# Local attention with a convolved feed-forward: attn @ v and scores of tile pairs as one TensorE step, on two lent PSUM banks

## The chip, the cores and the metric

The kernel runs on one core of a Trainium2 chip. A core has TensorE (PE in the profile; its weight loads are listed as PEld), VectorE (DVE), ScalarE (ACT), GpSimd (POOL) and SyncE (SP), which issues the DMAs here. The matrix products land in PSUM, which has eight banks of 512 fp32 columns on 128 partitions. The metric is device microseconds of one execution; the time of a kernel is the median of several runs.

## The reference

```
# q, k, v: 8 batches x 8 heads x 576 rows x 64;  d_model 512, d_ff 1024
chunk = 64                                  # attention inside chunks of 64 rows
scores = scale * q_c @ k_c^T
attn = exp(scores - max(scores))
attn = attn / (sum(attn) + 1e-9)
x = concat_heads(attn @ v_c)                # (8, 576, 512)

h = relu(x @ w_in)                          # (8, 576, 1024)
conv = sum over k in 0..2 of conv_w[k] * h shifted by k - 1 rows   # zero at the ends
out = (h * sigmoid(conv)) @ w_out           # (8, 576, 512)
```

All inputs and the output are fp32.

## The kernel before

**Tiles.** The 8 x 576 rows are cut in 36 tiles of 128 rows, two chunks of 64 rows with all 8 heads each. Of a tile, q and k come in transposed: up to tile 8 by PE transposes (`t_pe`, L144) and ACT copies, from tile 9 on by DVE (`t_dve`, L155). `scores` (L163) is a block of 16 matmuls of 64 x 64 x 64, which the profile lists as 32 records. Then come the maximum (`s_max`, DVE, L181), the subtraction (`s_sub`, DVE, L185), the exponential (ACT, L190), the sum, eps and reciprocal (DVE, L194 to L200), the product (POOL, L203), four PE transposes of the probabilities (`p_pe`, L210) with an ACT copy (L215), and `attn_v` (L217), another block of 16 small matmuls in 32 records. The result x, transposed, is split into a high and a low part: `x_hi` (ACT, L247) and `x_lo` (DVE, L251).

**Units.** The feed-forward runs on 16 units of 288 rows (half a batch). For each of the 8 slices of 128 features, `mm1` (L254) is a block of 12 matmuls (high x high, low x high, high x low, over 4 slices of d_model) with 290 columns. Its PSUM bank goes through `h_relu`, `c_mid` (ACT), `c_left`, `c_right` (DVE), `c_sig` (ACT) and `c_mul` (DVE, L290), which gives the bank back; `g_hi` (ACT) and `g_lo` (POOL, L304) split the gated rows. `mm2` (L309) multiplies by w_out: for each of 36 output tiles, 8 slices of 3 matmuls with 512 columns, all into one bank, which `o_copy` (ACT, L318) empties. The weights are split into high and low parts by DVE, ACT and POOL in the first part of the kernel (L327 to L379).

**PSUM.** `sx` is one tile of two banks, in two halves (`sx_half`, L160). A half holds the scores or the x of one tile, in 256 columns of both banks. Six more banks (`banks`) are shared by mm1, mm2 and all PE transposes.

**Order.** Every piece of work is a `step` with an engine, a cost, a due time (`key`), what must precede it, and the buffers that it takes and frees (`room`, L394). A planner (L583 to L677) goes through time and chooses, for each engine, the next step by due time. It adds a cost when PE turns between three kinds of work (`kinds`, `turn`: big matmuls, the small blocks of scores and attn_v, transposes), and it draws a small block to another one by six microseconds of due time (L632). Tables (`by_step_early` for due times under 110, `by_step`, `by_chain`) shift the due times. The instructions are then issued in the planned order, which each engine keeps. Where the plan leaves PE idle before the first mm2, filler transposes of the identity are put in (L685). In `att` (L424), a tile's chain of steps is written down from the load to `x_lo`.

Of the kernel before, what the change touches and what calls it, by code (L numbers as in the profile page):

```python
# [30 lines left out]
def attn_ffn(ctx: ExitStack, tc: tile.TileContext, q, k, v, w_in, conv_w, w_out, out):  # L31
    nc = tc.nc
# [17 lines left out]
    TG = 3  # L50
    scale = 1.0 / float(D) ** 0.5
# [108 lines left out]
    def sx_half(i):  # L160
        return sx[:, :, G * C * i:G * C * i + G * C]

    def scores(st):  # L163

        s_ps = sx_half(st["s"])
        qT, kT = st[0], st[1]
        for g in range(G):
            for s in range(2):
                for hp in range(2):
                    d0 = 64 * hp  # L170
                    nc.tensor.matmul(  # L171
                        s_ps[C * s:C * s + C, hp ^ s, C * g:C * g + C],
                        lhsT=qT[d0:d0 + D, g, C * s:C * s + C],
                        rhs=kT[d0:d0 + D, g, C * s:C * s + C],
                        start=True, stop=True,
                    )

    def s_max(st):
        st["sv"] = sx_half(st["s"]).rearrange("p u (g j) -> p u g j", j=C)
        st["m"] = work.tile([P, 2, G], F32, name="m")  # L180
        nc.vector.tensor_reduce(out=st["m"], in_=st["sv"], op=ALU.max, axis=AX.X)  # L181

    def s_sub(st):
        st["e"] = work.tile([P, H, C], F32, name="e")
        nc.vector.tensor_tensor(  # L185
            out=st["e"].rearrange("p (g u) j -> p u g j", u=2), in0=st["sv"],
            in1=st["m"].rearrange("p u (g o) -> p u g o", o=1).broadcast_to([P, 2, G, C]), op=ALU.subtract)
# [29 lines left out]
    def attn_v(st):  # L217
        x_ps = sx_half(st["x"])
        for g in range(G):
            for s in range(2):  # L220
                for hp in range(2):
                    j0 = 64 * (hp ^ s)
                    nc.tensor.matmul(  # L223
                        x_ps[D * hp:D * hp + D, s, C * g:C * g + C],
# [4 lines left out]

    def x_views(st, t, x):  # L230

        xv = sx_half(st.get("x", 0)).rearrange("p s (g i) -> p g s i", i=C)
# [7 lines left out]
        if [p[1:4] for p in parts] == [(0, C, parts[0][3])] * 2:  # L240
            _, _, _, u, o = parts[0]
            return [(xv, x[:, u, :, o:o + 2 * C].rearrange("p g (s i) -> p g s i", i=C))]
        return [(xv[:, :, s, i:i + n], x[:, u, :, o:o + n]) for s, i, n, u, o in parts]
# [150 lines left out]
    room = {"slot": 2, "wslot": 2, "sx": 2, "bk": 6, "grp": 2, "v": 4, "qT": 2, "kT": 2, "m": 2, "e": 2, "z": 2, "pT": 2, "c": 7, "wt": 2,  # L394
# [29 lines left out]
    def att(t, key, load_key, writes):  # L424
# [19 lines left out]
        s = step("PE", 0.47, key, scores, (st,), tt + [before.get("s")], take=[("sx", st, "s")], free=["qT", "kT"], bank="sx")  # L444
        before.update(v=ldv, T=tt[1], s=s)
# [8 lines left out]
        s = step("ACT", 0.59, key + 12, p_copy, (st,), [s], take=["pT"], free=[("bk", "pt")])  # L454
        s = step("PE", 0.47, key + 14, attn_v, (st,), [s, ldv], take=[("sx", st, "x")], free=["pT", "v"], bank="sx")
        n = len(x_views(st, t, x_h)) - 1
        s = step("ACT", 0.58 + 0.15 * n, key + 14, x_hi, (st, t), [s] + writes, bank="sx")
        return step("DVE", 0.69 + 0.1 * n, key + 14, x_lo, (st, t), [s], free=[("sx", "x")], bank="sx")

    group_loads, before = {}, {}  # L460
# [57 lines left out]

    for u in range(NU + 1):

        for t in tiles_for[u] if u < NU else []:
# [3 lines left out]
            x_done[t] = att(t, key_of[t], 0.1 + 0.5 * t if t < 5 else 4.5 + t, writes)  # L525
# [23 lines left out]
        "w_load": -4.5, "w_mask": -6, "w_bias": -5.5, "w_rest": -5, "w_low": -2, "w_sign": -9.5, "w_pow": -6,  # L549
        "<lambda>": -7, "c_sum": -23.5, "c_pe": 5, "c_copy": -31.5, "w_hi": 12, "w_lo_big": 20, "load_rows": -11,  # L550
        "t_pe": -7.5, "t_copy": -11, "load_v": 10.5, "scores": -3, "s_max": 8, "s_sub": -21.5, "s_exp": -9, "s_sum":
        -0.5, "s_eps": 2.5, "s_rec": 10, "s_norm": -19, "p_copy": -0.5, "attn_v": 4, "x_hi": -3, "x_lo": -6, "mm1":
        -0.5, "h_relu": -4.5, "c_mid": 2, "c_left": 2.5, "c_right": 2.5, "c_sig": 5, "c_mul": 6, "g_hi": 3, "g_lo":
        29.5, "o_copy": 6, "o_store": 16.5, "load_group": 35.5, "load_part": -3.5, "t_dve": 23
    }
    by_step = {
        "w_load": -4.5, "w_mask": -6, "w_bias": -5.5, "w_rest": -5, "w_low": -2, "w_sign": -9.5, "w_pow": -6,
        "<lambda>": -7, "c_sum": -23.5, "c_pe": 5, "c_copy": -31.5, "w_hi": 12, "w_lo_big": 20, "load_rows": -11,
        "t_pe": -7.5, "t_copy": -11, "load_v": 10.5, "scores": -3, "s_max": 8, "s_sub": -21.5, "s_exp": -9, "s_sum":
        -0.5, "s_eps": 2.5, "s_rec": 10, "s_norm": -19, "p_copy": -0.5, "attn_v": 4, "x_hi": -3, "x_lo": -6, "mm1":  # L560
        -0.5, "h_relu": -4.5, "c_mid": 2, "c_left": 2.5, "c_right": 2.5, "c_sig": 5, "c_mul": 6, "g_hi": 3, "g_lo":
        29.5, "o_copy": 6, "o_store": 16.5, "load_group": 35.5, "load_part": -3.5, "t_dve": 23
    }
    by_chain = [
# [155 lines left out]
```

## Time and profile before

| | |
|---|---|
| median of 3 runs | 516.65 us (516.14 to 516.67) |
| the profiled execution | 517.22 us |
| its span, first to last instruction | 515.4 us |
| TensorE clock granted, mean | 0.999 |
| mm2 matmuls (L313) | 864, 344.3 us busy in three groups |
| mm1 matmuls (L260) | 1536, 271.5 us busy in three groups |
| attn_v records (L223) and scores records (L171) | 1152 each, 24.5 and 24.3 us |
| filler transposes (L685) | 183, 26.0 us |
| DMA queue, share of the 16 engines | 40.5% |

The profile is of one execution. "Busy" of an engine counts its instructions' times without gaps; matmuls overlap, so the sums of the PE groups exceed the time that PE takes for them, and what a matmul costs is read from the distance between starts. A row of the timeline gives the start, the length, the engine, the line, the operation, its output and inputs, and how many neighbours it merges; a row of the waits gives who waited for whom, the total in us, how many times, and the longest.

### The profile page before, as it was taken

The page shows a single profiled execution, that of the slowest core. Times are in us where ns is not written, and L with a number is a line of the kernel's source. Part 1 is how long each engine was busy: PE and PEld are TensorE (multiplying, and loading weights), DVE is VectorE, ACT ScalarE, POOL GpSimd, SP SyncE. Part 2 cuts the span into 40 slices and gives each one's busy share as a digit, 9 for nine tenths or more (in the row PEclk, how much of TensorE's full clock was granted, in tenths as well). Part 3 has the DMA queues.
Part 4 walks back from the last instruction along what each step waited for, and adds up shares of the span by engine and source line. Part 5 has one row for each costly group of instructions (what it writes and reads, how often), then busy time and mean ns, then how long its engine had stood idle before and what let it go on. Part 6 is the DMA issues. An engine that isn't in the chain of part 4 may idle for free.

```text
span 515.4 us, 13095 instructions
## 1 busy us (share of the span) xinstructions
PE 505.4 (98%) x5104; PEld 450.8 (87%) x5104; DVE 351.8 (68%) x732; ACT 325.1 (63%) x783; POOL 172.1 (33%) x237
## 2 busy tenths in 40 slices
PE   8898999999999999999999999999999999999997
PEld 8788988888998899899888898889889898988985
DVE  5779999668749588867854499727858585753320
ACT  4678998845866367757635487737746567755430
POOL 1424485532314323532511153314313315043220
PEclk9999999999999999999999999999999999999999
DMA  8889751543325545523455554343551211001101
GB/s 218 198 218 262 187 131 37 93 100 88 51 46 117 89 114 108 98 47 51 100 114 113 123 89 85 57 97 74 97 121 33 61 23 42 2 1 43 41 14 68
DMA packets 183170, 47.04 MB, mean 91 GB/s; under 512 B 175404, under 2 KB 175428, under 8 KB 183108
## 3 DMA queue, kind: packets, MB, share of 16 engines
q1 hardware_dynamic: 183108, 46.20, 40.5%
q8 instruction: 40, 0.66, 0.6%
q14 instruction: 22, 0.18, 0.1%
HBM read 36.72 MB, written 9.44 MB: 90 GB/s over the span
## 4 chain that ended last, share of the span: by engine, by line
PE 85%; DVE 8%; DMA 3%; ACT 2%; POOL 1%; issue 0%; SPq 0%; DVEq 0%; ACTq 0%; POOLq 0%
PE b_ps L313 38%; PE b_ps L260 37%; PE sx_ps L223 4%; PE sx_ps L171 3%; DMA qk<-in_moe_w_in 3%; PE b_ps L210 3%; DVE wt L360 1%; DVE wv L355 1%; POOL wv L376 1%; DVE wv L351 1%; DVE we L368 1%; DVE c L281 1%; DVE wt L342 1%; DVE c L290 1%; DVE x_l L251 1%; DVE c L275 1%
## 5 line engine op out<-in xcount | busy, mean ns | idle before, releaser
L304 POOL TENSOR_TENSOR g_l<-c,g_h 128x288 fp32r<-128x288 f32 (+8 forms) x184 | 114.7, 638 | 217.3 <-ACT g_h L300 209.8
L313 PE MATMUL b_ps<-wo_h,g_h 128*128 128x512 f32 x288 | 118.1, 410 | 0.0
L313 PE MATMUL b_ps<-wo_h,g_l 128*128 128x512 f32 x288 | 113.3, 393 | 0.0
L313 PE MATMUL b_ps<-wo_l,g_h 128*128 128x512 f32 x288 | 112.9, 392 | 0.0
L275 DVE SCALAR_TENSOR_TENSOR c<-b_ps,cw,c 128x288 f32<-128x288 f32 (+1 forms) x128 | 65.2, 512 | 62.7 <-ACT c L271 62.4
L260 PE MATMUL b_ps<-x_h,wi_h 128*128 128x290 f32 x512 | 91.5, 300 | 1.3 <-DVE c L290 1.3
L260 PE MATMUL b_ps<-x_l,wi_h 128*128 128x290 f32 x512 | 90.2, 298 | 0.0
L260 PE MATMUL b_ps<-x_h,wi_l 128*128 128x290 f32 x512 | 89.8, 297 | 0.0
L260 PEld LDWEIGHTS b_ps<-x_h,wi_h 128*128 128x128 f32 x512 | 77.3, 189 | 6.2 <-DVE c L290 2.3
L266 ACT ACTIVATE b_ps<-b_ps 128x290 f32<-128x290 f32 x128 | 50.7, 398 | 47.1 <-PE b_ps L260 46.4
L300 ACT CAST g_h<-c 128x288 fp32r<-128x288 f32 (+8 forms) x184 | 60.3, 358 | 26.9 <-DVE c L290 13.3
L260 PEld LDWEIGHTS b_ps<-x_h,wi_l 128*128 128x128 f32 x512 | 76.4, 190 | 0.0
L260 PEld LDWEIGHTS b_ps<-x_l,wi_h 128*128 128x128 f32 x512 | 76.3, 189 | 0.0
L290 DVE SCALAR_TENSOR_TENSOR c<-c,b_ps 128x288 f32<-128x288 f32 x128 | 57.2, 449 | 20.5 <-ACT c L287 18.8
L287 ACT ACTIVATE c<-c 128x288 f32<-128x288 f32 x128 | 56.5, 443 | 22.7 <-DVE c L281 21.5
L281 DVE SCALAR_TENSOR_TENSOR c<-b_ps,cw,c 128x287 f32<-128x287 f32 (+1 forms) x128 | 65.4, 514 | 2.9
L271 ACT ACTIVATE c<-b_ps,cw 128x288 f32<-128x288 f32 x128 | 63.3, 498 | 4.7 <-POOL g_l L304 0.4
L313 PEld LDWEIGHTS b_ps<-wo_h,g_l 128*128 128x128 f32 x288 | 54.1, 188 | 12.2
L203 POOL TENSOR_TENSOR e<-e,z 128x512 f32<-128x512 f32 x36 | 38.1, 1062 | 75.8 <-DVE z L200 62.5
L313 PEld LDWEIGHTS b_ps<-wo_h,g_h 128*128 128x128 f32 x288 | 54.2, 188 | 10.3
L313 PEld LDWEIGHTS b_ps<-wo_l,g_h 128*128 128x128 f32 x288 | 54.2, 188 | 8.6
L181 DVE TENSOR_REDUCE m<-sx_ps 128x8 f32<-128x512 f32 x36 | 24.6, 683 | 22.3 <-PE sx_ps L171 21.4
(48 smaller groups left out, 513.1 us busy)
## 6 DMA issues: line engine op xcount, KB each, us to landing
v<-in_v SPq DMA_DIRECT2D x144, 64.0 KB, 2.6
out<-wt SPq DMA_DIRECT2D x36, 256.0 KB, 2.4
qk<-in_q SPq DMA_DIRECT2D x96, 48.0 KB, 2.3
qk<-in_k SPq DMA_DIRECT2D x96, 48.0 KB, 2.3
qk<-in_moe_w_out SPq DMA_DIRECT2D x4, 1024.0 KB, 7.7
qk<-in_q SPq DMA_DIRECT2D x96, 24.0 KB, 1.9
qk<-in_k SPq DMA_DIRECT2D x96, 24.0 KB, 1.9
qk<-in_moe_w_in SPq DMA_DIRECT2D x4, 512.0 KB, 5.1
```

Source lines behind the costliest of these rows:

```text
L181: nc.vector.tensor_reduce(out=st["m"], in_=st["sv"], op=ALU.max, axis=AX.X)
L203: nc.gpsimd.tensor_tensor(out=st["e"], in0=st["e"], in1=st["z"].rearrange("p (h o) -> p h o", o=1).broadcast_to([P, H, C]), op=ALU.mult)
L260: nc.tensor.matmul(h_ps[:, 0:XU], lhsT=wt[:, f // 2, kt, P * (f % 2):P * (f % 2) + P], rhs=xt[:, u % NX, kt, :], start=n == 0, stop=n == 3 ...
L266: nc.scalar.activation(out=banks[st["h"]][:, 0:XU], in_=banks[st["h"]][:, 0:XU], func=AF.Relu)
L271: nc.scalar.mul(out=st["c"], in_=banks[st["h"]][:, i0:i0 + HS], mul=cw[:, FT + f:FT + f + 1])
L275: nc.vector.scalar_tensor_tensor(out=c[:, a:HS], in0=banks[st["h"]][:, i0 + a - 1:i0 + HS - 1], scalar=cw[:, f:f + 1], in1=c[:, a:HS], op0 ...
L281: nc.vector.scalar_tensor_tensor(out=c[:, 0:b], in0=banks[st["h"]][:, i0 + 1:i0 + 1 + b], scalar=cw[:, 2 * FT + f:2 * FT + f + 1], in1=c[: ...
L287: nc.scalar.activation(out=st["c"], in_=st["c"], func=AF.Tanh, scale=0.5)
L290: nc.vector.scalar_tensor_tensor(out=st["c"], in0=st["c"], scalar=1.0, in1=banks[st["h"]][:, st["i0"]:st["i0"] + HS], op0=ALU.add, op1=ALU ...
L300: nc.scalar.copy(out=g_h[:, f, gs], in_=st["c"][:, cs])
L304: nc.gpsimd.tensor_tensor(out=g_l[:, f, gs], in0=st["c"][:, cs], in1=g_h[:, f, gs].bitcast(F32), op=ALU.subtract)
L313: nc.tensor.matmul(banks[st["o"]], lhsT=gt[:, f, o:o + P], rhs=wt[:, f, :], start=f == 0 and n == 0, stop=f == FT - 1 and n == 2)
```

## The change

Tiles 0 to 11 keep a step each for scores, and tiles 0 to 10 for attn_v. From tile 12 on, two tiles (12 and 13, 14 and 15, ...) are taken together: `both` is one step of PE that holds attn_v of the two tiles before (in the first one, of tile 11 alone) and then scores of the two new ones. Attn_v of tiles 34 and 35 is one last step. Softmax (`soft`) and the split of x (`x_steps`) stay steps of single tiles.

The four blocks need four places. From tile 11's scores on, two of the six shared banks are taken for good (`give_up`, which issues nothing) and make two more halves, numbers 0 and 1; halves 2 and 3 are the old `sx`. As a lent pair is two separate tiles, `sx_half` returns two views there, and `s_max`, `s_sub`, `x_hi` and `x_lo` issue an instruction for each bank.

Units of x are now filled in when mm1 first needs them (the loop with `begun`). All tables of due times are replaced; the one for due times of 110 and more is empty. Fillers may stand wherever the plan leaves PE idle up to 110 us. A bank that is not given back counts as held to the end.

```
+    BOTH = 12
+    PAIR = 12
...
     def sx_half(i):
-        return sx[:, :, G * C * i:G * C * i + G * C]
+        cols = slice(G * C * (i % 2), G * C * (i % 2) + G * C)
+        if i // 2:
+            return [(slice(0, 2), sx[:, :, cols])]
+        return [(slice(u, u + 1), banks[lent["y", u]].rearrange("p (u n) -> p u n", u=1)[:, :, cols]) for u in range(2)]
+
+    def sx_bank(i, u):
+        parts = sx_half(i)
+        return parts[0][1][:, u, :] if len(parts) == 1 else parts[u][1][:, 0, :]
...
     def s_max(st):
-        st["sv"] = sx_half(st["s"]).rearrange("p u (g j) -> p u g j", j=C)
         st["m"] = work.tile([P, 2, G], F32, name="m")
-        nc.vector.tensor_reduce(out=st["m"], in_=st["sv"], op=ALU.max, axis=AX.X)
+        for us, sv in sx_half(st["s"]):
+            nc.vector.tensor_reduce(out=st["m"][:, us], in_=sv.rearrange("p u (g j) -> p u g j", j=C), op=ALU.max, axis=AX.X)
...
+    def both(st, tiles, tiles_x):
+        for a in tiles_x:
+            attn_v(a)
+        for a in tiles:
+            scores(a)
...
-    room = {"slot": 2, "wslot": 2, "sx": 2, "bk": 6, "grp": 2, "v": 4, "qT": 2, "kT": 2, "m": 2, "e": 2, "z": 2, "pT": 2, "c": 7, "wt": 2,
+    room = {"slot": 2, "wslot": 2, "sx": 4, "bk": 6, "grp": 2, "v": 4, "qT": 2, "kT": 2, "m": 2, "e": 2, "z": 2, "pT": 2, "c": 7, "wt": 2,
...
-        s = step("PE", 0.47, key, scores, (st,), tt + [before.get("s")], take=[("sx", st, "s")], free=["qT", "kT"], bank="sx")
-        before.update(v=ldv, T=tt[1], s=s)
+        before.update(v=ldv, T=tt[1])
+        before["new"].append((st, t, tt, ldv, writes, key))
+        if t >= PAIR and (t - PAIR) % 2 == 0:
+            return
+        new, old = before["new"], before["x"] if t >= BOTH else []
+        before["new"], key = [], new[0][5]
+        after = [a for n in new for a in n[2]] + [before.get("s")] + [a for o in old for a in o[2]]
+        take = [("sx", o[0], "x") for o in old] + [("sx", n[0], "s") for n in new]
+        free = ["qT", "kT"] * len(new) + ["pT", "v"] * len(old)
+        if old:
+            s = step("PE", 0.47 * len(new + old), key, both, (new[0][0], [n[0] for n in new], [o[0] for o in old]), after,
+                     take=take, free=free, bank="sx")
+        else:
+            s = step("PE", 0.47, key, scores, (st,), after, take=take, free=free, bank="sx")
+        before["s"] = s
+        for b, tb, _, writes_b in old:
+            x_steps(b, tb, s, key, writes_b)
+        if t == PAIR - 1:
+            a = step("POOL", 0.0, key, give_up, (lent,), [s], take=[("bk", lent, ("y", 0))])
+            step("POOL", 0.0, key, give_up, (lent,), [a], take=[("bk", lent, ("y", 1))], free=[("sx", "l0"), ("sx", "l1")])
+        before["x"] = [(st_, t_, soft(st_, s, key + 4 * n) + [v_], w_) for n, (st_, t_, _, v_, w_, _) in enumerate(new)]
+        if t + 1 < BOTH:
+            x_alone(key + 14)
+        elif t == NT - 1:
+            x_alone(key + 18)
...
-        for t in tiles_for[u] if u < NU else []:
+        while begun < NT and u < NU and not all(t in x_done for t in range(until[u])):
+            t, begun = begun, begun + 1
...
-    kinds = {scores: 1, attn_v: 1, p_pe: 2, t_pe: 2, c_pe: 2}
+    kinds = {scores: 1, attn_v: 1, both: 1, p_pe: 2, t_pe: 2, c_pe: 2}
...
-    pe_free, until_ = 2.0, min(begin[i] for i in range(n_) if steps[i]["fn"] is mm2)
+    pe_free, until_ = 2.0, 110.0
```

78 lines of the change are left out of this document (44 added, 34 removed), and 19 rows, old and new, of the table by_chain.

## The prediction

> **What bounds the kernel now.** The page comes first: the span, the engines' shares, the slices, and the chain that ended last.
>
> ```profile
> span 515.4 us, 13095 instructions
> ...
> PE 505.4 (98%) x5104; PEld 450.8 (87%) x5104; DVE 351.8 (68%) x732; ACT 325.1 (63%) x783; POOL 172.1 (33%) x237
> ...
> PE   8898999999999999999999999999999999999997
> ...
> PEclk9999999999999999999999999999999999999999
> ...
> PE 85%; DVE 8%; DMA 3%; ACT 2%; POOL 1%; issue 0%; SPq 0%; DVEq 0%; ACTq 0%; POOLq 0%
> ```
>
> The reader is to see one full engine. TensorE (PE) is busy for 98% of the span, it holds 85% of the chain, and its clock is full from end to end. The rest of the chain is VectorE (DVE), ScalarE (ACT) and DMA. The next two views say where that rest lies: the busy time by stretches (columns: us, then PE, PEld, DVE, ACT, POOL busy with their instructions, clock, DMA share, GB/s), and the list of waits of PE from 60 us on.
>
> ```profile
> 40.00:60.00 20.00, 18.22 (x224) 17.25 (x223) 19.50 (x37) 18.77 (x42) 9.23 (x8) 1.00 0.83 218
> 60.00:80.00 20.00, 19.50 (x176) 17.36 (x175) 19.85 (x40) 18.58 (x39) 15.24 (x10) 1.00 0.59 146
> ...
> 160.00:515.40 355.40, 351.61 (x3417) 311.84 (x3416) 225.65 (x479) 208.65 (x530) 107.31 (x165) 1.00 0.33 71
> ```
>
> ```profile
> PE b_ps L260 <- DVE c L290: 0.5, 1, 0.5
> ```
>
> Up to about 80 us DVE is the full engine (19.50 and 19.85 of 20 us; the weights are split there). From 160 us on PE is busy 351.61 of 355.40 us, and the missing 3.8 us is the last copy and store, after the last matmul. After 60 us PE waits for another engine once, for 0.5 us. So from 80 us on the time is simply what PE has to do, in whatever order. A microsecond taken from PE there comes off the end; one of DVE, ACT or DMA costs nothing until it makes PE wait.
>
> **What the change removes: turns of PE into the small matmuls and back.** A busy share does not show what such a turn costs; the starts do. In the timeline of PE, the last two matmuls of mm2 before a single scores block, the block, and two matmuls after it (first column: start):
>
> ```profile
> 187.62 0.40 PE L313 MATMUL b_ps<-wo_l,g_h 128*128 128x512 f32 x1
> 187.85 0.40 PE L313 MATMUL b_ps<-wo_h,g_l 128*128 128x512 f32 x1
> 188.18 0.69 PE L171 MATMUL sx_ps<-kT,qT 64*64 64x64 f32 x32
> 188.80 0.51 PE L313 MATMUL b_ps<-wo_h,g_h 128*128 128x512 f32 x1
> 189.15 0.40 PE L313 MATMUL b_ps<-wo_l,g_h 128*128 128x512 f32 x1
> ```
>
> And the same around scores with an attn @ v right behind it:
>
> ```profile
> 264.40 0.39 PE L313 MATMUL b_ps<-wo_l,g_h 128*128 128x512 f32 x1
> 264.63 0.40 PE L313 MATMUL b_ps<-wo_h,g_l 128*128 128x512 f32 x1
> 264.95 0.69 PE L171 MATMUL sx_ps<-kT,qT 64*64 64x64 f32 x32
> 265.47 0.65 PE L223 MATMUL sx_ps<-pT,v 64*64 64x64 f32 x32
> 266.05 0.50 PE L313 MATMUL b_ps<-wo_h,g_h 128*128 128x512 f32 x1
> 266.39 0.39 PE L313 MATMUL b_ps<-wo_l,g_h 128*128 128x512 f32 x1
> ```
>
> Inside a stretch of mm2 the starts are 0.23 us apart (264.40 to 264.63). From 187.85 to 189.15 are 1.30 us; less two matmuls of mm2 (0.46) the single block costs 0.84 us. From 264.63 to 266.39 are 1.76 us; less 0.46 the two blocks cost 1.30 us. So a second block in the same run costs 0.46 us, and the run itself 0.84 - 0.46 = 0.38 us: the matmul before it (0.32 for 0.23), its own end, and the first matmul after it (0.34 for 0.23) are all drawn out.
>
> How many runs go? In the trace these are the first and the last of the 28 separate runs that hold scores and attn @ v of tiles 12 to 35 (48 blocks: 20 pairs, 5 scores alone, 3 attn @ v alone); attn @ v of tile 11 shares a 29th run with tile 10's, which stays:
>
> ```profile
> 160.74 0.69 PE L171 MATMUL sx_ps<-kT,qT 64*64 64x64 f32 x32
> ...
> 464.37 0.39 PE L313 MATMUL b_ps<-wo_h,g_l 128*128 128x512 f32 x1
> 464.69 0.69 PE L223 MATMUL sx_ps<-pT,v 64*64 64x64 f32 x32
> 465.32 0.51 PE L313 MATMUL b_ps<-wo_h,g_h 128*128 128x512 f32 x1
> 465.66 0.40 PE L313 MATMUL b_ps<-wo_l,g_h 128*128 128x512 f32 x1
> ```
>
> The last one gives the price again: 1.29 - 0.46 = 0.83 us alone, so 0.37 us for the run; I take 0.37. In the changed code these blocks stand in 13 steps: one of three blocks (attn @ v of tile 11, a second block there as here, and scores of 12 and 13), eleven of four, and one of two at the end (attn @ v of 34 and 35). 28 - 13 = 15 runs go: 15 x 0.37 = 5.5 us off PE. No run of more than two blocks is in the trace. Its third and fourth block cost at least what the second does (nothing is left to save) and at most what a single one does, 0.84; I take 0.46, as the second block already follows a full block. Up to tile 11 the steps stay single. How often two of them fall together depends on the new order; one or two runs more or fewer are 0.4 to 0.7 us either way, and I take nothing.
>
> **What it adds on DVE and ACT.** Scores or x in one of the two lent banks pairs are two views, one for each bank, so the maximum, the subtraction, x_hi and x_lo become two instructions of half the size. What halving costs is in the groups by shape:
>
> ```profile
> L185 DVE TENSOR_TENSOR e<-sx_ps,m 128x512 f32<-128x512 f32 x36 | 24.9, 691 | 3.1 <-PE b_ps L210 0.8
> L181 DVE TENSOR_REDUCE m<-sx_ps 128x8 f32<-128x512 f32 x36 | 24.6, 683 | 22.3 <-PE sx_ps L171 21.4 <-PE sx_ps L223 0.8
> ...
> L251 DVE TENSOR_TENSOR x_l<-sx_ps,x_h 128x512 fp32r<-128x512 f32 x24 | 16.6, 691 | 13.5 <-ACT x_h L247 13.3
> ...
> L251 DVE TENSOR_TENSOR x_l<-sx_ps,x_h 128x256 fp32r<-128x256 f32 x16 | 6.4, 419 | 1.8 <-ACT x_h L247 1.6
> ```
>
> Two halves of x_lo are 2 x 0.419 = 0.84 us in place of 0.69: 0.15 us more; I take the same for the others. With two of a step's four uses in lent banks that is at most 2 x 2 x 0.15 = 0.6 us of DVE per step, 7 us in all. DVE has 355.4 - 225.65 = 130 us free from 160 us on, so the end doesn't see it. ACT has more room and gets less. Loads, stores and PE transposes keep their number; one wait for all four blocks' inputs is new, and the softmax of a tile has a whole round between two steps (some 355 / 12 = 30 us) to be ready for it.
>
> **What it gives up: two of six banks.** From tile 11's scores to the end, mm1, mm2 and the transposes of the probabilities share four banks. An mm1 bank is held from the first matmul to c_mul. In the stretch of eight mm1 blocks that begins at 435.55:
>
> ```profile
> 435.55 0.78 PE L260 MATMUL b_ps<-x_h,wi_h 128*128 128x290 f32 x4
> ...
> 438.88 0.71 PE L260 MATMUL b_ps<-x_h,wi_h 128*128 128x290 f32 x4
> ...
> 440.54 0.44 DVE L290 SCALAR_TENSOR_TENSOR c<-c,b_ps 128x288 f32<-128x288 f32 x1
> ...
> 445.30 0.46 DVE L290 SCALAR_TENSOR_TENSOR c<-c,b_ps 128x288 f32<-128x288 f32 x1 [0.53 <-ACT c L287]
> 445.36 0.70 PE L260 MATMUL b_ps<-x_h,wi_h 128*128 128x290 f32 x4
> ```
>
> The first block holds its bank from 435.55 to 440.98, 5.4 us; the third from 438.88 to 445.76, 6.9 us. Blocks start (445.36 - 435.55) / 6 = 1.63 us apart. With four banks the seventh would ask at 445.36 for the third one's bank and wait 0.4 us; with one of the four held by an mm2 tile, the fourth block (at 435.55 + 3 x 1.63 = 440.44) waits 0.5 us for the first, and each later one about as long as holds exceed 3 x 1.63 = 4.9 us, 0.5 to 2.0. So eight-block stretches no longer fit, and short ones with mm2 between, which needs one bank for 24 x 0.23 = 5.5 us of PE, do. The order is new and can do that, as no work is tied to a long stretch. The bounds: nothing if it does (fewer banks free nothing earlier, so no gain), and one stretch of eight per round with waits of 0.5 us in five blocks, 12 x 5 x 0.5 = 30 us, if it keeps the old habit. The nearest row of PE that does wait for c_mul is the 0.5 us above; I take a little more than that one wait, 0.8 us. The Trainium skill (Perfetto Trace Analysis, Optimization Strategy) says that the same gap repeating on the engine that should be full can mean too little PSUM for the next tile. In this trace there is no such gap, so six banks were enough; whether four are is the rule against this change, the first rival.
>
> **The sum.** 5.5 us off, 0.8 us back: 4.7 us. The profiled execution took 517.2 us, 1.8 us beyond its span, and lies 0.57 us above the median; 517.2 - 4.7 = 512.5 against it, and 512.0 us against the median of 516.65.
>
> **The rivals.**
> First, slower: PE waits for banks. Behind a step of four blocks DVE has two maxima, two subtractions and two x_lo to do, 2 x (0.68 + 0.69 + 0.69) = 4.1 us, and any c_left or c_mul queued behind them gives its bank back that much later. With four banks PE then stands. It decides at 5.5 / 12 = 0.46 us of wait per round; at 1 us per round the time is 516.65 - 5.5 + 12 = 523. For it: the holds above, already longer than four banks allow in a long stretch. Against it: DVE is busy 63% and ACT 59% from 160 us on, and mm2 can lie behind the step. 0.13.
>
> Second, no difference: the first 80 us take the gain back. Their order is new too, and fillers may now stand up to a planned 110 us. There DVE is full, so moving an attention instruction ahead of a weight moves the whole rest. The stretch 40 to 80 us has 1.78 + 0.50 = 2.3 us of idle PE, and fillers besides:
>
> ```profile
> 40.00:60.00 20.00, 2.29 (x16) 1.79 (x16) 1.00 0.83 218
> ```
>
> That is 4.6 us in which PE does nothing of use. A better order could win up to these 4.6 us, a worse one lose about as much: 512.0 + 4.6 = 516.6. 0.09.
>
> Third, the same stretch is won, in part or whole: 512.0 - 4.6 = 507.4 at most, 509.7 at half. 0.15.
>
> Fourth, the four blocks don't run on as the second does, so that the change doesn't do what it says. If the third and fourth cost 0.84 each, 23 blocks lose 0.38: 8.7 us, more than the gain, 520.7. Against it, the second block shows no start-up of its own. The Trainium skill (TensorE: Matmul & The Clock Gate, the part on the array's architectural detail) gives PE a queue of 64 instructions, so a longer run could outlast it. A run of two has 64 matmul records and as many loads, twice that, and kept its pace. 0.03.
>
> **How the numbers follow.** The forecast has 0.60, with its own range 509.5 to 514.5 (0.8 us of waits replaced by 0 to 3, and the early order by 1.5 us either way). About 0.2% (1.0 us) is what a measurement of this kernel can tell from no change. Below 515.6 lie the forecast and the third rival and a part of the second: 0.77. Within 0.2% the rest of the second: 0.07. Above lie the first and fourth: 0.16. The range, 508.5 to 517.5, leaves out those two and the best of the third.
>
> **What would show it.** After 110 us PE should have 13 runs of small matmuls from tile 12 on, most of them with 128 records and about 1.30 + 2 x 0.46 = 2.2 us from the last mm2 matmul's regular end to the next one's. Waits of PE for DVE c (L290's c_mul) should stay about 1 us. The starts of the last mm2 stretch should come some 5 us earlier, while the first mm1 and the fillers end where they did. It is wrong if PE waits for c_mul or for the o_copy by more than 5 us in total, if the first regular mm2 stretch starts later by several us, or if the third and fourth block are spaced wider than the second.

## The result, and the profile after

| | before | after |
|---|---|---|
| median | 516.66 us (4 runs, 516.14 to 516.73) | 513.7 us (4 runs, 513.47 to 514.4) |
| the profiled execution | 517.22 us | 513.61 us |
| its span | 515.4 us | 511.8 us |
| filler transposes | 183, the last at 59.5 us | 175, the last at 66.4 us |

The changed kernel takes 0.9947 of the time (95% interval 0.9934 to 0.9959): 3.0 us less, where 4.7 less were forecast. One execution of 984.96 us (of the version with 79 us of before, further down) and one of 607.48 us (of the second move) were in a slow state: the medians given for these two versions count them, the ratios do not. The page, with the same lines as of before:

```profile
span 511.8 us, 13118 instructions
...
PE 500.9 (98%) x5096; PEld 450.6 (88%) x5096; DVE 352.4 (69%) x763; ACT 325.7 (64%) x792; POOL 171.3 (33%) x237
...
PE 86%; DVE 8%; ACT 2%; DMA 1%; POOL 1%; issue 1%; SPq 0%; DVEq 0%; ACTq 0%; POOLq 0%
```

PE is still the one full engine and holds 86% of the chain for 85%. DVE has 31 instructions more and only 0.6 us more of busy time. So the gain has to be looked for where the forecast put it, in the starts of PE. A four-block step in the timeline of PE (first column: start):

```profile
268.49 0.40 PE L334 MATMUL b_ps<-wo_h,g_l 128*128 128x512 f32 x1
268.81 0.69 PE L238 MATMUL sx_ps<-pT,v 64*64 64x64 f32 x32
269.33 0.65 PE L238 MATMUL b_ps<-pT,v 64*64 64x64 f32 x32
269.79 0.65 PE L186 MATMUL b_ps<-kT,qT 64*64 64x64 f32 x32
270.26 0.65 PE L186 MATMUL sx_ps<-kT,qT 64*64 64x64 f32 x32
270.84 0.50 PE L334 MATMUL b_ps<-wo_h,g_h 128*128 128x512 f32 x1
271.17 0.39 PE L334 MATMUL b_ps<-wo_l,g_h 128*128 128x512 f32 x1
```

The third block starts 0.46 us after the second, the fourth 0.47 after the third. From 268.49 to 271.17 are 2.68 us; less two matmuls of mm2 (0.46) the step costs 2.22, the forecast's 2.2. There are 13 such steps from tile 12 on, as forecast.

Two more things changed in the row of small blocks, ahead of tile 12. First the runs of scores and attn @ v of before between 95 and 160 us (of a run of two the second is left out), then those of after:

```profile
107.93 0.69 PE L171 MATMUL sx_ps<-kT,qT 64*64 64x64 f32 x32
110.83 0.69 PE L223 MATMUL sx_ps<-pT,v 64*64 64x64 f32 x32
117.19 0.69 PE L171 MATMUL sx_ps<-kT,qT 64*64 64x64 f32 x32
120.31 0.69 PE L171 MATMUL sx_ps<-kT,qT 64*64 64x64 f32 x32
...
123.09 0.69 PE L171 MATMUL sx_ps<-kT,qT 64*64 64x64 f32 x32
139.63 0.69 PE L223 MATMUL sx_ps<-pT,v 64*64 64x64 f32 x32
145.03 1.16 PE L223 MATMUL sx_ps<-pT,v 64*64 64x64 f32 x64
```

```profile
113.81 0.69 PE L238 MATMUL sx_ps<-pT,v 64*64 64x64 f32 x32
...
118.10 0.69 PE L238 MATMUL sx_ps<-pT,v 64*64 64x64 f32 x32
...
138.54 0.69 PE L186 MATMUL sx_ps<-kT,qT 64*64 64x64 f32 x32
...
152.79 0.69 PE L238 MATMUL b_ps<-pT,v 64*64 64x64 f32 x32
```

Before has seven runs here; after has three, and at 152.79 the first of the 13 steps. The new order pairs the single steps of tiles 7 to 11 too. So from 95 us on not 15 but 19 runs went: 7 + 28 = 35 became 3 + 13 = 16. Over the whole kernel it is 16: 48 runs became 32, as ahead of 95 us the changed kernel has 16 runs, each of one block, and before 13 runs with 15 blocks. One of the 19 has only moved ahead: scores of tile 8 stand at 107.93 in before and at 92.48 us in the changed kernel. The other change lies further ahead. First the first mm1 block of before, then that of after, with what stands ahead of it (in brackets: idle time of PE, and who ended it):

```profile
37.07 0.78 PE L260 MATMUL b_ps<-x_h,wi_h 128*128 128x290 f32 x4
```

```profile
39.02 0.69 PE L186 MATMUL sx_ps<-kT,qT 64*64 64x64 f32 x32 [0.45 <-DVE z L213]
39.64 0.80 PE L281 MATMUL b_ps<-x_h,wi_h 128*128 128x290 f32 x4
```

The first mm1 block comes 2.57 us later. **One yardstick** tells the two parts of the time apart. I count PE's work at the distance between starts inside a stretch: 0.135 us for a matmul of mm1, 0.2295 for one of mm2, 0.0147 for a small record, 0.109 for a transpose of q, k or the probabilities, nothing for a filler. The early part ends at the start of the matmul with which 60 us of such work are reached, which places it to one matmul, some 0.13 us; the later part goes from there to the start of the last matmul:

| profile | early part ends | last matmul | later part |
|---|---|---|---|
| before | 95.09 | 511.21 | 416.12 |
| before, another execution | 94.15 | 510.36 | 416.21 |
| after | 96.47 | 507.25 | 410.78 |
| after, another execution | 96.37 | 507.07 | 410.70 |

In the later part, which repeats to 0.1 us, 5.3 to 5.5 us went; in the early part 1.4 to 2.2 came back. What PE waits for from 60 us on (in us, times, longest), where before had one wait of 0.5:

```profile
PE b_ps L281 <- DVE c L311: 0.8, 1, 0.8
PE sx_ps L186 <- DVE x_l L272: 0.5, 1, 0.5
PE b_ps L281 <- ACT qT L155: 0.4, 1, 0.4
PE b_ps L226 <- POOL e L219: 0.3, 1, 0.3
```

There is one wait for a bank's c_mul, 0.8 us, the size that was taken. But it is not the wait that was meant:

```profile
72.57 0.81 PE L281 MATMUL b_ps<-x_h,wi_h 128*128 128x290 f32 x4 [0.76 <-DVE c L311]
```

It stands in the early part, and the two banks are given up only with tile 11's scores, at 138.54 us. The second and third row of the list stand at 60.2 and 61.3 us. Of the four only the last, 0.3 us for the product of the softmax, lies in the later part, where before's PE waits for no other engine.

### The profile page after: what moved, and what is told of

It is laid out like the page before. It is cut to its first block, busy times and chain, and to the rows that moved or that the text cites. A ratio compares the mean times of both kernels' runs of the same rounds, so it can differ in the third digit from the quotient of the medians.

```text
span 511.8 us, 13118 instructions
## 1 busy us (share of the span) xinstructions
PE 500.9 (98%) x5096; PEld 450.6 (88%) x5096; DVE 352.4 (69%) x763; ACT 325.7 (64%) x792; POOL 171.3 (33%) x237
## 4 chain that ended last, share of the span: by engine, by line
PE 86%; DVE 8%; ACT 2%; DMA 1%; POOL 1%; issue 1%; SPq 0%; DVEq 0%; ACTq 0%; POOLq 0%
PE b_ps L334 38%; PE b_ps L281 38%; PE b_ps L226 3%; PE sx_ps L186 2%; PE sx_ps L238 2%; PE b_ps L238 2%; DMA qk<-in_moe_w_in 1%; PE b_ps L186 1%; DVE wt L381 1%; DVE wv L376 1%; DVE wt L363 1%; DVE we L389 1%; DVE c L302 1%; DVE c L296 1%; DVE m L196 1%
## 5 line engine op out<-in xcount | busy, mean ns | idle before, releaser
L325 POOL TENSOR_TENSOR g_l<-c,g_h 128x288 fp32r<-128x288 f32 (+8 forms) x184 | 113.5, 630 | 216.2 <-ACT g_h L321 201.0
L281 PEld LDWEIGHTS b_ps<-x_h,wi_h 128*128 128x128 f32 x512 | 78.8, 189 | 8.5 <-DVE c L311 1.8
L339 ACT ACTIVATE wt<-b_ps 128x512 f32<-128x512 f32 x36 | 21.4, 596 | 32.8 <-PE b_ps L334 32.7
## 6 DMA issues: line engine op xcount, KB each, us to landing
qk<-in_moe_w_in SPq DMA_DIRECT2D x4, 512.0 KB, 5.2
```

The lines of the kernel that those rows point to most:

```text
L281: nc.tensor.matmul(h_ps[:, 0:XU], lhsT=wt[:, f // 2, kt, P * (f % 2):P * (f % 2) + P], rhs=xt[:, u % NX, kt, :], start=n == 0, stop=n == 3 ...
L325: nc.gpsimd.tensor_tensor(out=g_l[:, f, gs], in0=st["c"][:, cs], in1=g_h[:, f, gs].bitcast(F32), op=ALU.subtract)
L339: nc.scalar.mul(out=st["os"], in_=banks[st["o"]], mul=0.5)
```

## The experiments

The theory after the result: (A) each run of small blocks costs 0.36 us of PE wherever it stands, 19 went from 95 us on, and about 2 us of this are given back, most of it by the new order of the early part. The rivals: (B) the later part is shorter because the new order is better as such, with fewer waits, and not because of the four-block step; (C) the loss ahead of 80 us is the price of the change (lent banks, halves) or a difference between executions, and not of the order. Of single steps of the early order, more below.

**The step cut in two.** Everything as in the changed kernel, the order of all steps too, but the scores of a `both` step are issued behind the next big matmul step.

```
     def both(st, tiles, tiles_x):
         for a in tiles_x:
             attn_v(a)
-        for a in tiles:
-            scores(a)
+        later.extend(tiles)
...
         steps[i]["fn"](*steps[i]["args"])
+        while later and steps[i]["fn"] in (mm1, mm2):
+            scores(later.pop(0))
```

> The changed kernel, except that in the twelve steps that hold attn @ v and scores the scores are issued after the next big matmul step (one mm1 block or three matmuls of mm2), so that each of these runs falls into two. Nothing else moves, and all four blocks, banks and places stay. My theory (a run of small matmuls costs PE 0.37 us beyond its blocks, and that is where the change gains): 12 more runs, 12 x 0.37 = 4.4 us more than the changed kernel, about 518.1 us, which is slower than before. The rival (the gain comes from the new order as a whole, and the runs hardly matter): within 1 us of the changed kernel's 513.7.

It took 521.74 us, 1.010 of before (1.0087 to 1.0114): 8 us more than the changed kernel, where 4.4 were expected. The cut step in the timeline of PE:

```profile
272.19 0.40 PE L336 MATMUL b_ps<-wo_h,g_l 128*128 128x512 f32 x1
272.51 0.69 PE L241 MATMUL sx_ps<-pT,v 64*64 64x64 f32 x32
273.03 0.65 PE L241 MATMUL b_ps<-pT,v 64*64 64x64 f32 x32
273.60 0.50 PE L336 MATMUL b_ps<-wo_h,g_h 128*128 128x512 f32 x1
273.94 0.39 PE L336 MATMUL b_ps<-wo_l,g_h 128*128 128x512 f32 x1
...
274.49 0.69 PE L186 MATMUL b_ps<-kT,qT 64*64 64x64 f32 x32
275.01 0.65 PE L186 MATMUL sx_ps<-kT,qT 64*64 64x64 f32 x32
```

From 272.19 to 273.94 are 1.75 us; less 0.46 a run of two costs 1.29, two of them 2.58, and the run of four 2.22: 0.36 us for the cut. With twelve cuts these are 4.3 us, which is theory A's price measured in the changed order itself, where nothing but the place of the scores differs. The sum over the whole later part says the same: at the small runs and inside them the starts exceed the yardstick by 10.0 us in 28 runs here and by 5.6 in the changed kernel's 16, 4.4 us more. The other 4 us are mostly waits that the cut brings with it, since scores come later in an order that was made without the delay. Two rows of PE's waits from 60 us on:

```profile
PE b_ps L229 <- POOL e L222: 2.1, 3, 1.0
...
PE b_ps L229 <- DVE c L313: 0.6, 1, 0.6
```

The transposes of the probabilities now wait for the softmax (2.1 us for 0.3). Summed over all stretches of these transposes, PE loses 4.2 us around them where the changed kernel loses 1.3. So the expected time failed, as it left out these waits, and the time by itself proves nothing against B; the rows do: the cut alone costs what the turns were said to cost. Against B there is the yardstick as well. In the later part of before the starts at and inside the 35 small runs exceed it by 12.3 us, in the changed kernel those of 16 runs by 5.6: 0.35 us a run in both, 6.7 us less. Everything else exceeds it by 0.9 us in before and by 2.3 in the changed kernel. So the new order did not bring fewer waits there, but some more.

**Both kernels again, and the early order exchanged.** The changed kernel and the kernel before were run again as they are, beside versions with the early order exchanged. In the first of these the changed kernel issues on each engine what before issues in its first 79 us, in that order, and then goes on in its own. In the second only the first 37 us are taken from before. In the third it is the other way round: before, with what the changed kernel issues in its first 80 us. All three set the order by a list for each engine:

```
+    forced = {"PE": [...], "DVE": [...], "ACT": [...], "POOL": [...], "SP": [...]}
...
         for e, cand in ready.items():
-            picks = []
+            picks, cand = [], [i for i in cand if not forced[e] or i == forced[e][0]]
```

Before again:

> The kernel before, for a second profile. Its first profiled execution took 517.2 us, 0.57 above the median, while that of the changed kernel lay 0.1 below its median. If the half microsecond is chance in the first 80 us (loads of weights), the matmul that ends the common early part (the 24th of mm2 and the 15th mm1 block done) comes at 78.5 us rather than 79.0 and everything behind it keeps its length of 436.4 us. If it lies in the later part, the start stays at 79.0 and the later part is shorter.

After again:

> The changed kernel, for a second profile and time on the chip on which the others run: 513.7 us, within 0.5. The early part should end at 80.5 us again, if its place is set by the order, and anywhere from 79.5 to 81.5 if chance sets it.

The first 79 us of before:

> The changed kernel with the first 79 us in the order of the kernel before on every engine (all steps that its plan began before 79 us), and from there on the changed kernel's own order. At the end of that stretch PE has done the same matmuls in both kernels (15 blocks of mm1, 24 matmuls of mm2, scores of tiles 0 to 7, attn @ v of 0 to 4), the kernel before at 79.0 us of its trace and the changed one at 80.5. My theory (the new early order costs 1.5 us): 513.7 - 1.5 = 512.2 us. The rival (the two early orders are worth the same, and the 1.5 us are the chance of one execution's loads): 513.7, within 0.4.

The first 37 us of before:

> The changed kernel with only the first 37 us in the order of the kernel before (up to the first mm1 block, which starts at 37.1 us there and at 39.6 us in the changed kernel). If what the new early order loses is lost before the first mm1 block: about 512.0 us, as with the whole early part restored. If it is lost while weights and the first units compete for DVE, from 37 to 80 us: nearer to 513.5.

Before, with the first 80 us of after:

> The reverse: the kernel before, its first 80 us in the changed kernel's order on every engine, and its own order from there on. Six banks throughout, no steps of tile pairs. If the early order costs 1.6 us by itself: 516.5 + 1.6 = 518.1 us. If it costs only together with what follows in the changed kernel: 516.5, within 0.5. The seam between the two orders may add a wait of some tenths.

| | median | ratio to before | early part ends | later part |
|---|---|---|---|---|
| before again | 516.53 us | 1.0004 (0.9995 to 1.0012) | 94.15 | 416.21 |
| after again | 513.42 us | 0.9943 (0.9922 to 0.9964) | 96.37 | 410.70 |
| after, 79 us of before | 512.0 us | 0.9919 (0.9902 to 0.9937) | 94.71 | 410.72 |
| after, 37 us of before | 511.82 us | 0.9907 (0.9889 to 0.9925) | 95.11 | 410.70 |
| before, 80 us of after | 518.75 us | 1.0055 (1.0033 to 1.0078) | 96.53 | 416.10 |

The last column takes two values only, 416.1 to 416.2 and 410.7, whatever order stands in front. That separates the two parts. With an early order of before, the changed kernel's early part ends 1.3 to 1.8 us sooner (94.71 and 95.11 against 96.37 and 96.47), and the first 37 us give most of it. Both of these versions have the lent banks, the halves and the four-block step, and the banks are lent only at 138.54 us, behind the early part: as the price of these, C falls. What of it is a difference between executions comes next. The version with 37 us of before is the fastest kernel of this study: 4.9 us faster than before, 1.6 to 1.9 faster than the changed kernel.

That the order alone costs those 1.3 to 1.8 us is not shown. Before with the changed kernel's first 80 us issues the same instructions in the same order as the changed kernel up to there, and yet is 1.2 us ahead of it from x_lo of tile 0 on. First the changed kernel's row, then that of before with the 80 us:

```profile
25.02 0.69 DVE L272 TENSOR_TENSOR x_l<-sx_ps,x_h 128x512 fp32r<-128x512 f32 x1 [1.61 <-ACT x_h L268]
```

```profile
23.48 0.69 DVE L251 TENSOR_TENSOR x_l<-sx_ps,x_h 128x512 fp32r<-128x512 f32 x1
```

In the changed kernel's profile the granted clock of PE is 0.50 from 20.0 to 23.4 us; the transposes and fillers there are drawn out, and attn @ v of tile 0 starts at 23.64 us. In the other the clock is 1.00 and it starts at 22.05; the first mm1 block follows at 39.64 and at 38.40. The scores block that waits 0.54 us for an x_lo comes at 60.21 in the changed kernel, at 59.01 in before with the 80 us, and at 58.87 with the first 37 us of before: at full clock the order of the first 37 us shows in these profiles as 0.14 us. The second profile of the changed kernel has the low clock too, the profiles of the two versions with before's early order have not.

The runs say that the clock is not all of it. Of the changed kernel's eleven (the first four and the seven of after again) six have a mean clock of 0.995 to 0.997 and a median of 514.0 us, five have 0.998 to 1.0 and 513.3; the eleven with before's early order all have at least 0.998, and a median of 511.8. In the one session that holds both kinds, after again has 514.1 us in four runs of the low clock and 512.4 in three others, and the version with 79 us of before 511.6 in five. So 0.7 to 1.7 us go with the low clock, and 0.8 to 1.5 are left. Whether the order brings the low clock about is not shown; the kernel before has it in some of its runs as well.

In the last row of the table, 2.1 us slower than the 516.7 beside it, there is a seam besides:

```profile
86.38 0.69 PE L223 MATMUL sx_ps<-pT,v 64*64 64x64 f32 x32 [1.35 <-DVE x_l L251]
```

Neither of the two kernels has this wait of 1.35 us; it comes behind the exchanged stretch, where the one order passes into the other. Without it the early part would end up to 1.35 us sooner, at some 95.2 us, which is 0.1 to 1.0 behind before's own.

**Two banks less and nothing else.** What the gift of two banks costs where it isn't paid back: the kernel before, planned again with two of the six banks taken from tile 11's scores on, its due times kept, its steps single.

```
+        if t == 11:
+            a = step("POOL", 0.0, key, give_up, (lent,), [s], take=[("bk", lent, ("y", 0))])
+            step("POOL", 0.0, key, give_up, (lent,), [a], take=[("bk", lent, ("y", 1))])
```

> The kernel before, except that from tile 11's scores on two of the six shared banks are taken away and used by nothing; its due times are kept, and the order follows from them with four banks. This is the giving up alone, without the steps of tile pairs and without an order made for it. My theory (four banks are enough only where the order is made for them): PE waits for c_mul and o_copy in most rounds, 10 to 30 us more than before, 527 to 547. The rival (four banks are enough in any order): 516.5, within 1.

It took 535.6 us, 1.0368 of before (1.0342 to 1.0394), 19 us more. PE's own matmuls show only a part of these waits as idle time; its weight loads (PEld), which wait for the same bank, show them best. First this kernel, then before, from 60 us on:

```profile
PEld b_ps L263 <- DVE c L293: 15.4, 31, 1.9
```

```profile
PEld b_ps L260 <- DVE c L290: 1.3, 3, 0.9
```

31 waits for c_mul in place of 3, 14.1 us more, by far the largest row. PE's own list has only 4.7 us for the same wait, so they are not PE's time one for one. The plan for four banks also breaks up four more runs of small blocks (39 from 95 us on for 35). How the 19 us divide stays open. But the first rival of the prediction was a real danger: with due times made for six banks, the kernel with four loses well more than the turns bring. The Trainium skill (Perfetto Trace Analysis, Optimization Strategy) takes a gap that keeps coming back on the full engine as a sign that PSUM may be too small for the next tile; this profile agrees, with these 31 waits. Once the banks are lent, the changed kernel waits for c_mul only in its loads, once, 0.35 us at 192.35. Its longest stretch of mm1 after tile 12 is six blocks (308.4 to 318.1 us) where before has eight, and most are one to three; that this is why four banks do was not tried.

**Twice the halves.** All views of the changed kernel are split by bank from tile 11 on, those of the old `sx` too, in its own order.

```
     def sx_half(i):
...
+        if i // 2 and "on" in lent:
+            return [(slice(u, u + 1), sx[:, u:u + 1, cols]) for u in range(2)]
...
     def give_up(st):
-        pass
+        st["on"] = 1
```

> The changed kernel in its own order, except that from tile 11's scores on the maximum, the subtraction, x_hi and x_lo are issued one bank at a time for the old pair of banks as well: about two times the added instructions. About 24 uses of two DVE instructions at 0.15 us more each, some 7 us more of DVE and 3 of ACT. My theory (they hide behind PE): 513.5 us, within 0.5. The rival (DVE's extra work holds banks longer, and with four of them PE waits): 1 to 5 us more.

It took 513.96 us, 0.9947 of before (0.9926 to 0.9967), the changed kernel's ratio. The stretch from 160 us on (us, then PE, PEld, DVE, ACT, POOL busy, clock, DMA share, GB/s), first of the changed kernel, then with twice the halves:

```profile
160.00:511.80 351.80, 347.27 (x3390) 312.40 (x3388) 225.20 (x510) 214.10 (x553) 108.79 (x168) 1.00 0.33 71
```

```profile
160.00:511.80 351.80, 347.40 (x3390) 312.44 (x3388) 226.85 (x541) 214.88 (x561) 109.08 (x168) 1.00 0.33 71
```

31 more DVE instructions are 1.65 us more of DVE, where some 7 were expected: a split costs DVE 0.05 us, as the halves overlap, and not 0.15. So this is a smaller load than was meant. At the end 0.3 us of it can be seen at most (its later part is 411.0 us for 410.7 to 410.8): that work is covered, as forecast.

**Which step of the first 37 us?** Three places stood out in the changed kernel's trace. DVE's short instructions are drawn out beside GpSimd's; here two of DVE, then GpSimd's own:

```profile
29.94 0.76 DVE L213 TENSOR_SCALAR z<-z 128x8 f32<-128x8 f32 x1
...
32.63 1.12 DVE L403 TENSOR_TENSOR wt<-wt,we 24x128 f32<-24x128 f32 x1
```

```profile
29.39 1.28 POOL L397 TENSOR_TENSOR wv<-wv,we 128x512 f32<-128x512 f32 x1 [1.71 <-DVE we L389]
32.56 1.04 POOL L219 TENSOR_TENSOR e<-e,z 128x512 f32<-128x512 f32 x1 [1.89 <-DVE z L216]
```

Then the scores of tile 4 ahead of the first mm1 block, shown above, and a wait of DVE of 1.61 us for x_hi of tile 0. The first was moved away, the second, and then all three together, in the changed kernel's order and with nothing else changed:

```
 DVE:  s_sum a2, s_eps a2, w_mask, w_rest, x_lo a1, w_low, w_sign, w_pow, s_rec a2, (w0), c_sum, s_max a3
  to:  s_sum a2, x_lo a1, s_eps a2, w_mask, w_rest, w_low, w_sign, w_pow, (w0), c_sum, s_rec a2, s_max a3
 PE:   attn_v a2, scores a4, mm1 (first)      to:  attn_v a2, mm1 (first), scores a4
 DVE:  x_lo a0, w_rest, s_rec a1, w_low       to:  w_rest, s_rec a1, w_low, x_lo a0
```

The first move alone:

> The changed kernel with two moves in VectorE's order at 29 to 33 us and nothing else: x_lo of tile 1 goes ahead of eps of tile 2, and the reciprocal of tile 2 goes behind the product of the conv weights' preparation (c_sum). In the changed kernel's profile two short VectorE instructions are drawn out there, each beside a GpSimd instruction: eps of tile 2 takes 0.76 us for 0.17 (GpSimd busy 29.39 to 30.67), and c_sum takes 1.12 us for 0.28 (GpSimd busy 32.56 to 33.60). The moves put instructions that read PSUM beside GpSimd's. Theory A (these 1.4 us are what the new early order loses): x_lo of tile 2 comes 1 to 1.4 us earlier than 38.04, the first mm1 block as well, and the kernel takes 512.1 to 512.7 us for the changed kernel's 513.5. Theory B (the first mm1 block is late because scores of tile 4 stand ahead of it, or because of the wait in front of x_lo of tile 0): no change, 513.2 to 513.8.

The second alone:

> The changed kernel with one move in TensorE's order and nothing else: scores of tile 4 go behind the first mm1 block instead of ahead of it. Theory B: the first mm1 block starts at about 39.0 us for 39.64 and the kernel takes 512.5 to 513.0 us. Theory A (VectorE's drawn-out instructions set the pace): the block starts earlier by up to 0.6 us but scores of tile 4 come later by as much, and the time stays at 513.2 to 513.8.

All three:

> Both of these moves, and x_lo of tile 0 three instructions later on VectorE, so that the 1.61 us in which VectorE waits for x_hi of tile 0 has work in it. If the losses of the early part lie in these three places, the first mm1 block starts at about 37.0 to 37.6 us for 39.64, and the kernel takes 511.8 to 512.3 us, as the version with the kernel before's first 37 us did (511.8). If the time stays above 513, the loss lies elsewhere in the first 37 us.

| | median | ratio to before | first mm1 block | early part ends | later part |
|---|---|---|---|---|---|
| first move | 512.74 us | 0.9929 (0.9916 to 0.9943) | 39.85 | 96.72 | 410.70 |
| second move | 513.14 us | 0.9930 (0.9917 to 0.9944) | 38.39 | 96.87 | 410.71 |
| all three | 513.93 us | 0.9950 (0.9938 to 0.9963) | 39.34 | 97.08 | 410.70 |

None of them ends the early part sooner than the changed kernel does (96.37 to 96.47). The medians of the first two are 0.3 to 1.0 us below its 513.42 and 513.7, with intervals that overlap its own, and that of all three together is not below. But here too the clock differs from run to run: the first move's three runs at a mean clock of 0.998 or more took 512.7 us, its two others 513.8; of all three moves four of the five runs lie below 0.998. So these medians cannot tell the order of single steps from the clock. The first move did what it was made for, in the rows of DVE:

```profile
30.63 0.69 DVE L272 TENSOR_TENSOR x_l<-sx_ps,x_h 128x512 fp32r<-128x512 f32 x1 [0.92 <-ACT x_h L268]
31.24 0.16 DVE L213 TENSOR_SCALAR z<-z 128x8 f32<-128x8 f32 x1
...
32.99 0.28 DVE L403 TENSOR_TENSOR wt<-wt,we 24x128 f32<-24x128 f32 x1
```

0.16 and 0.28 us instead of 0.76 and 1.12, 1.44 us of DVE won; but x_lo of tile 1, moved ahead, now waits 0.92 us for ACT, and x_lo of tile 2 comes at 38.25 for 38.04. The second move brought the first mm1 block forward by 1.25 us, and PE had not got further at the end of the early part. The third place, the 1.61 us of DVE, is shown above: it is the wait that the low clock makes, and it is not there in before with the 80 us. What costs the 0.8 to 1.5 us at full clock stays open. The one profile at full clock with the changed kernel's own order up to the first mm1 block is that of the step cut in two. It is 1.13 us ahead of the changed kernel at scores of tile 4 (37.89 for 39.02) and loses it right behind them, in a wait that the profile puts to no engine ("issue"):

```profile
39.58 0.81 PE L283 MATMUL b_ps<-x_h,wi_h 128*128 128x290 f32 x4 [0.99 <-issue]
```

Whether the other runs at full clock have that wait isn't known.

## Why the prediction was right, and where it was off

**What bounds the kernel.** Right: from about 95 us on the time is what PE has to do. The split step put its work on PE and it came out at the end; of 1.65 us more on DVE at most 0.3 did.

**The turns.** The price was right (0.37 taken; 0.36 measured by the cut), and so was the count of 13 steps. The step "up to tile 11 the steps stay single ... I take nothing" holds for the count, 20 runs before and 19 after, but not for where they stand: the new order has two more of them ahead of 60 us, where fillers show that PE has time to spare, one more at 92.48 us, and four fewer behind 95 us, where each one counts. So 19 x 0.36 = 6.8 us stand in place of 5.5 in the later part. The code doesn't tell this; it hangs on the planned order.

**The third and fourth block.** Taken at 0.46, measured at 0.46 and 0.47, at the lower bound. The fourth rival falls, and so does what it drew from a queue of 64: a run of 128 records keeps the pace of one of 64.

**DVE and ACT.** Right in that it is hidden; taken at 0.15 us a split, from the lengths of single instructions. Groups of the changed kernel by shape: a half of the maximum, of the subtraction and of x_lo takes

```profile
L272 DVE TENSOR_TENSOR x_l<-b_ps,x_h 128x256 fp32r<-128x256 f32 x24 | 9.1, 413 | 0.0
L196 DVE TENSOR_REDUCE m<-b_ps 128x4 f32<-128x256 f32 x22 | 8.3, 417 | 6.9 <-PE b_ps L186 6.9
L201 DVE TENSOR_TENSOR e<-b_ps,m 128x256 f32<-128x256 f32 x22 | 8.1, 411 | 0.0
```

0.41 to 0.42 us, two of them 0.14 to 0.15 more than the whole (0.68 to 0.69). So the lengths came as taken, but the halves overlap in time: by the busy time of twice the halves a split costs DVE 0.05 us.

**The banks.** The 0.8 us taken and the 0.8 us in PE's list agree by luck. The wait stands at 72.57 us, ahead of the lending, and before with the changed kernel's first 80 us, which lends none, has it too (0.78 us at 71.37). From the lending on PE waits for no bank. That the new order can do with four, as the prediction held possible, is borne out. What it did not take is that the later part loses time elsewhere: it is 5.3 to 5.5 us shorter, not 6.8, so 1.3 to 1.5 are lost there. About 1.0 of it stands around the transposes of the probabilities that have no small run beside them (28 stretches of them exceed PE's pace by 1.28 us in sum, 20 in before by 0.30). PE's list names 0.3 of it, POOL's product; in the list of the weight loads from 145 us on the transposes wait 1.8 us for POOL, in before 0.3. The rest, some 0.4 us, lies inside the stretches of mm2 and where they pass into mm1; its cause is open.

**The early order.** This is the term that was off in size: taken at 0, with 1.5 us either way inside the forecast, and a rival at the whole 4.6. The early part ended 1.4 to 2.2 us later in the profiles, and 1.3 to 1.8 us of it went with an early order of before. It is the main reason why the gain is 3.0 and not 4.7 us. But the second rival's mechanism, an attention instruction that is moved ahead of a weight, is not what the runs show. Some 0.35 us of the 1.4 to 2.2 is the run of scores that moved ahead of the boundary; in the two profiles of the changed kernel the low clock of 20.0 to 23.4 us makes some 1.2; beside these two the profiles leave little, but the runs at full clock are still 0.8 to 1.5 us above those with before's early order, and the cause of that stays open. The errors partly cancel: 4.7 forecast, 1.3 more from the turns, 0.6 more lost in the later part, 1.4 to 2.2 lost ahead, which makes 3.2 to 4.0; the last matmul came 3.3 to 4.0 us earlier in the two pairs of profiles, and the medians give 3.0.

**The range.** The forecast's own range, 509.5 to 514.5, is narrower at the top than its terms: 516.65 - 5.5 with 0 to 3 us of waits and 1.5 either way goes from 509.7 to 515.7. The 513.7 lies in both.

**What would show it.** Of the signs named, the 13 runs of 2.2 us came, and the waits for c_mul stayed about 1 us (0.8, none of it from the lending on). "The last mm2 stretch some 5 us earlier, while the first mm1 and the fillers end where they did" did not: the last matmul came 3.96 us earlier, the first mm1 2.57 us later, and the last filler at 66.4 us for 59.5.

## What to carry to other kernels

Where one engine is full, count the runs of each kind of work in the order as it is issued, over the whole stretch in which that engine has no time to spare and not only where the change is written, and price a run by the starts around it: that gave 2.22 us for a step that was not in any trace. When a change comes with a new order, treat each stretch of the kernel that the change did not need as a term of its own with its own sign, and afterwards exchange just that stretch between the two kernels; here it gave 1.6 us that no look at single steps had found. Before such a difference is put down to the order, look at the granted clock of every profile and every run, and at the seam: both stood in these numbers. And look where a wait stands, not only how long it is: a wait of the forecast size came ahead of what was to cause it. Two banks given up cost no wait of PE for a bank in an order that was made for four; under the old due times the kernel with four took 19 us longer.

## What the runs showed of the hardware that was not expected

- A run of 64 x 64 matmuls between 128 x 128 ones costs 0.36 us however long it is. The Trainium skill (TensorEngine Tiling (Array Packing), Tiling Modes, Key Properties) says that a change of the tiling mode, but not one of the tile within a mode, drains the engine. The rows agree: the change between attn @ v and scores, which moves banks and operands but not the mode, costs nothing (0.46 to 0.47 us a block, with it or without), and each pair of changes of the mode costs 0.36.
- Short DVE instructions on SBUF lasted until GpSimd's instruction beside them ended (0.76 for 0.16 us, 1.12 for 0.28), and moved out from beside it they took their own time. One that reads PSUM did not: in the kernel with the first move GpSimd's product runs from 33.55 to 34.59, and the subtraction of tile 3, which starts beside it at 33.97, takes its usual 0.69 us. For the product of two SBUF inputs this is as the Trainium skill (SBUF — State Buffer, SBUF: two separate sides) has it, where such a DVE instruction and a GpSimd one hold a shared port in turn.
- The granted clock of PE was 0.50 for 3.4 us around 19 to 23 us in some executions of the same program and 1.00 throughout in others: low in five of the eight profiles with the changed kernel's early order (the moves among them), at full in the two of before and the two with before's early order. The stretch of 20 to 40 us (columns as above), first of the changed kernel, then of the kernel with the step cut in two, whose early order is the same:

```profile
20.00:40.00 20.00, 18.59 (x300) 16.61 (x299) 17.90 (x42) 13.65 (x27) 6.68 (x6) 0.92 0.82 201
```

```profile
20.00:40.00 20.00, 17.44 (x302) 15.08 (x301) 19.38 (x43) 14.22 (x27) 6.78 (x6) 1.00 0.90 218
```

  The early part ended at 96.47 in the first and at 96.42 in the second, but this does not show that the clock costs nothing: the second was 1.13 us ahead at scores of tile 4 and lost 0.99 behind them, as shown above. Between the changed kernel and before with its first 80 us, at 1.00, the distance of 1.2 us stays up to the wait for c_mul at 72.57 and 71.37.
- The early part of one and the same kernel differs by 0.94 us between two executions (95.09 and 94.15), while the later part repeats to 0.1 us.
